# A two-stage kernel (a gated recurrence and a mixer): one group of small products a unit, keys' transposes ahead of products with v, and decays from one scan over logarithms from unit 6 on

## Chip, cores and metric

The kernel runs on one core of a Trainium2 chip. TensorE (PE, with its weight loads as PEld), VectorE (DVE), ScalarE (ACT), GpSimd (POOL) and SyncE (SP, which issues DMAs) each work through a queue of their own. The metric is the device time of one execution in microseconds. All data are float32.

## What is computed

The reference runs a gated outer-product recurrence over 768 steps for 4 batches and 8 heads of 48 channels, and puts its output, as a 768 x 384 matrix a batch, through a mixer:

```python
f = 1.0 / (1.0 + np.exp(-f_logit))
for t in range(S):
    state = f[:, :, t, :, None] * state + np.einsum('bhd,bhe->bhde', k[:, :, t], v[:, :, t])
    y[:, :, t] = np.einsum('bhd,bhde->bhe', q[:, :, t], state)
...
h = xt @ U @ V
u = x + h.transpose(0, 2, 1)
ch = np.maximum(u @ w_ch1, 0.0) @ w_ch2
return (u + ch)
```

## The kernel before

**Units.** Two heads make a unit, four units a batch, so units 0 to 15; unit n is in batch n // 4. The 768 steps are cut into 12 chunks of 64. Channels lie on partitions, head 0 at 0 to 47 and head 1 at 64 to 111. Within a chunk the recurrence becomes products: with decays X (from a step to the chunk's end) the keys become k·X, with Y = 1/X the queries become q·Y. These are the steps of a unit.

- `gates`, `keep`, `keys`, `read_back`, `queries` (function `prepare`, the "front") make f, X, k·X, Y and q·Y. `keep` is the backward scan at L876 on DVE over products of f, with a maximum (L883), a reciprocal (L884) and the chunk's whole decay (L886) behind it; `read_back` is the forward scan at L894. From unit 6 on (`TURNED`) f, k and q come in with channels in 32x32 blocks and are turned by DVE (L754); before that TensorE turns them (L777). Batch 0 has another way, from logarithms by products with a triangle (L835), which the change leaves as it is but for one copy.
- `kept` (function `attend`, the "rear") turns k·X back on TensorE (`pt`, L1002) and copies it to `kb` on ACT (L1006); `spread` copies the chunks' whole decays 48 times (L1012).
- `states` makes k·v a chunk (`ds`, L1026) and copies it to `added` on ACT (L1034); `scan` runs over the 12 chunks on DVE (L1051) and puts the states into `st`, on POOL (L1057) or ACT (L1055).
- `scores` makes k·q a chunk (`sc`, L975), masked on DVE to `A` (L988).
- `read` makes q·state (`y`, L1069); `inner` adds A·v to it (L1087) and ACT copies y into the mixer's x (L1093).

All of these products are small for TensorE: 48 or 64 rows and 48 to 128 columns of its array. A unit's y, ds, sc, pt (and others) are PSUM tiles of the pool `ps_big`, which has three buffers.

**The mixer.** One batch behind, the mixer's large products fill TensorE: `pz` (L300) with w_ch1, and with w_ch2 `po` (L355) in batch 0, `pw` (L389) with fewer products in the others, `pp` (L495) at the end. DVE makes the sums that these need (L204 in `add`, and L929 for sums of weights, at places given by `turns`).

**Order.** TensorE's order is the program's. `steps(first, last)` yields pieces of attention; before each piece a `Fill` emits its share of the mixer's pieces, so the number of pieces between two groups sets how many large products stand there. A piece made by `joined` runs several steps at once, with an empty piece ahead for each group of steps but one. Until the start of batch 2's mixing DVE's and ACT's orders are the program's as well; behind that, and for POOL throughout, a planner orders instructions by priority and by when they can start. The weights come in as 64-bit numbers and are converted on ACT (L91, L92), DVE (L98 to L100) and POOL (L101), one load beside each early piece of batch 1.

Before, a unit n has two groups: inner of n-2, scores of n-1 and kept of n together, and later read of n-1 and states of n together.

Of the kernel before, what the change touches and what calls it, by code (L numbers as in the profile page):

```python
# [564 lines left out]
def factored_path(ctx, tc, q, k, v, f_logit, moe_U, moe_V, moe_w_ch1, moe_w_ch2, out, ok):  # L565
# [154 lines left out]
    for i in range(2):  # L720
        nc.gpsimd.memset(wholes[i][:, 0:1], 0.0)
# [38 lines left out]
    def prepare(n):  # L760
# [5 lines left out]
        by_chunk = f[:, 0:S].rearrange("p (c t) -> p c t", t=C)  # L766
# [73 lines left out]
        def keep_logs():  # L840
# [16 lines left out]
            nc.scalar.copy(wholes[n % 2][:, 1:NCH], least[:, n, 1:NCH])  # L857

        def gates():
            f0 = T["f0"] = two.tile([P, NCH], F32, name="f0")  # L860
            if n < TURNED:
                pt = on_tensor("f")
                nc.scalar.activation(halves(f)[:, :, :, 1:C], pt[:, :, :, 1:C], AF.Sigmoid)
# [7 lines left out]
            nc.scalar.activation(by_chunk[:, :, 1:C], fv[:, :, 1:C], AF.Sigmoid)  # L871
            nc.scalar.activation(f0, fv[:, :, 0], AF.Sigmoid)

        def keep():
            X = T["X"] = late[:, 4, :]
            nc.vector.tensor_tensor_scan(  # L876
# [8 lines left out]
            whole = wholes[n % 2]  # L885
# [71 lines left out]
    def attend(n):  # L957
# [58 lines left out]

        def states():

            M = D if b else PAD
            ds = ps_big.tile([P, 2, 512], F32, name="ds", tag="big")  # L1020
            for c in range(NBL):
                for s in range(2):
                    for par in range(2):
# [3 lines left out]
                            ds[par * PAD : par * PAD + M, s, c * D : (c + 1) * D],  # L1027
                            lhsT=T["kb"][part[s ^ par], par, i, 0:M], rhs=vt[part[s ^ par], c, par, :],
# [3 lines left out]
            for r in rows if b else [slice(0, P)]:  # L1032
# [6 lines left out]
        def scan():  # L1039
# [8 lines left out]
            with tc.high_priority(offset=2 * AHEAD):  # L1048
                for e in halves_of(n):
                    of = slice(e.start * NCH, e.stop * NCH)  # L1050
                    nc.vector.tensor_tensor_scan(  # L1051
                        states[:, of], added[:, of], T["whole"].rearrange("p e c -> p (e c)")[:, of], 0.0, ALU.add, ALU.mult
# [46 lines left out]
        return [kept, states, scan, scores, read, inner, mask, spread]  # L1099
# [12 lines left out]
    def rear(n, *names):  # L1112
# [3 lines left out]
        if n not in here:  # L1116
            here[n] = dict(zip(("kept", "states", "scan", "scores", "read", "inner", "mask", "spread"), attend(n)))
# [10 lines left out]
    def steps(first, last):  # L1128

        def behind(n):  # L1130

            return HP + 3 <= n < NU - 1

        for n in range(first, last):
            if n < NU:
                yield from joined(rear(n - 2, "inner"), rear(n - 1, "scores"), rear(n, "kept"))
            else:
                for piece in rear(n - 2, "inner") + rear(n - 1, "scores"):
                    yield lambda: None
                    yield piece  # L1140
            if behind(n):
                yield from front(n, "read_back", "queries")
            if n + 1 < NU and n + 1 not in v_tiles:
                load(n + 1, "v")
            yield from front(n + 1, "gates", "keep", "keys")
            yield from joined(rear(n - 1, "read"), rear(n, "states", "scan"))
            if not behind(n + 1):
                yield from front(n + 1, "read_back", "queries")
            if n + 1 == last:
                yield from rear(n - 1, "inner")  # L1150
                if n + 2 < NU:
                    load(n + 2, "v")

# [160 lines left out]
    turns = 5, 7, 8, 13, 14, 15, 16, 18, 19, 22, 27  # L1314
# [6 lines left out]
    attention(pieces, Fill(todo[:-1], 33))  # L1321
# [373 lines left out]
```

## Time and profile before

| | |
|---|---|
| median of 3 runs | 466.35 us (465.92 to 467.19) |
| span of the profiled execution | 463.2 us |
| PE busy | 455.2 us, 98%, 5639 instructions |
| PEld busy | 394.5 us, 85% |
| DVE busy | 351.4 us, 76%, 585 instructions |
| ACT busy | 170.4 us, 37%, 323 instructions |
| POOL busy | 48.5 us, 10%, 56 instructions |
| granted TensorE clock, mean | 0.999 |

The span goes from the first to the last instruction of the profiled execution; the runs' times are of other executions and hold what lies around the span too. A busy PE is not PE at its peak: the ends of matmuls are modelled, and matmuls overlap, so the starts of rows say more than their lengths. In a timeline row stand the start, the length, the engine, the line, the operation, out<-in, shapes and the count of instructions merged; in brackets the idle time in front and what ended it. A float32 product is two instructions in the count, a transpose is one.

### The profile page before, as it was taken

The page shows a single profiled execution, that of the slowest core. Times are in us where ns is not written, and L with a number is a line of the kernel's source. Part 1 is how long each engine was busy: PE and PEld are TensorE (multiplying, and loading weights), DVE is VectorE, ACT ScalarE, POOL GpSimd, SP SyncE. Part 2 cuts the span into 40 slices and gives each one's busy share as a digit, 9 for nine tenths or more (in the row PEclk, how much of TensorE's full clock was granted, in tenths as well). Part 3 has the DMA queues.
Part 4 walks back from the last instruction along what each step waited for, and adds up shares of the span by engine and source line. Part 5 has one row for each costly group of instructions (what it writes and reads, how often), then busy time and mean ns, then how long its engine had stood idle before and what let it go on. Part 6 is the DMA issues. An engine that isn't in the chain of part 4 may idle for free.

```text
span 463.2 us, 13016 instructions
## 1 busy us (share of the span) xinstructions
PE 455.2 (98%) x5639; PEld 394.5 (85%) x5639; DVE 351.4 (76%) x585; ACT 170.4 (37%) x323; POOL 48.5 (10%) x56
## 2 busy tenths in 40 slices
PE   8999999999999999999999999999999999999997
PEld 5886888875666578999898888899989999999996
DVE  6778788979999677676765559977797887858652
ACT  6785776562333143323322323451412311212200
POOL 2002445634112001010000000000000000000000
PEclk9999999999999999999999999999999999999999
DMA  9959997577777604504633030100000000000001
GB/s 194 186 139 212 227 217 180 150 119 103 124 113 118 107 18 53 78 1 89 77 52 74 14 61 4 28 3 21 18 1 1 35 1 23 13 1 35 1 36 39
DMA packets 148583, 34.35 MB, mean 74 GB/s; under 512 B 136934, under 2 KB 146982, under 8 KB 148518
## 3 DMA queue, kind: packets, MB, share of 16 engines
q1 hardware_dynamic: 147718, 33.29, 37.1%
q8 instruction: 46, 0.75, 0.7%
q10 hardware_dynamic: 800, 0.15, 0.2%
q14 instruction: 19, 0.16, 0.1%
HBM read 28.70 MB, written 4.72 MB: 72 GB/s over the span
## 4 chain that ended last, share of the span: by engine, by line
PE 80%; DVE 11%; ACT 3%; DMA 2%; issue 2%; SPq 2%; DVEq 0%; ACTq 0%
PE pw L389 27%; PE pz L300 21%; PE pp L495 12%; PE po L355 5%; PE y L1069 2%; PE sc L975 2%; PE ds L1026 2%; PE y L1087 2%; PE pt L1002 1%; SPq L661 1%; DVE late L894 1%; PE pt L777 1%; DVE late L876 1%; PE pt L835 1%; DMA other<-in_f_logit_dram 1%
## 5 line engine op out<-in xcount | busy, mean ns | idle before, releaser
L300 PE MATMUL pz<-uT,w 128*128 128x256 f32 x492 | 111.5, 382 | 0.3
L300 PEld LDWEIGHTS pz<-uT,w 128*128 128x128 f32 x492 | 91.7, 190 | 12.9 <-ACT uT L289 0.6
L389 PE MATMUL pw<-zw,w_raw 128*128 128x192 f32 x216 | 38.0, 329 | 0.0
L389 PE MATMUL pw<-w,z_all 128*128 128x192 f32 x216 | 37.3, 327 | 0.0
L335 ACT ACTIVATE z_all<-pz 128x512 f32<-128x512 f32 x33 | 19.6, 598 | 45.1 <-PE pz L300 44.7
L389 PEld LDWEIGHTS pw<-w,z_all 128*128 128x128 f32 x216 | 35.3, 190 | 0.5
L389 PEld LDWEIGHTS pw<-zw,w_raw 128*128 128x128 f32 x216 | 35.1, 190 | 0.6 <-issue 0.3
L101 POOL TENSOR_TENSOR w<-w_y,w_r 128x384 int32<-128x384 int32 x24 | 31.5, 1311 | 37.0 <-DVE w_y L100 22.5
L876 DVE TENSOR_TENSOR_SCAN late<-fz,late 128x768 f32<-128x768 f32 x12 | 21.1, 1755 | 9.4 <-ACT fz L871 9.3
L488 ACT ACTIVATE other<-other 128x512 f32<-128x512 f32 x18 | 11.3, 630 | 40.3 <-DVE other L204 40.3
L355 PE MATMUL po<-w,zw 128*128 128x384 f32 x72 | 25.2, 495 | 0.0
L355 PE MATMUL po<-w,z_all 128*128 128x384 f32 x72 | 24.7, 493 | 0.0
L1057 POOL COPY st<-added 128x576 f32<-128x576 f32 x8 | 12.4, 1556 | 113.8 <-DVE added L1051 113.8
L988 DVE TENSOR_TENSOR A<-sc,causal 128x768 f32<-128x768 f32 x16 | 15.2, 953 | 8.5 <-PE sc L975 8.5
L355 PEld LDWEIGHTS po<-w,zw 128*128 128x128 f32 x72 | 13.2, 190 | 9.6 <-issue 0.8
L894 DVE TENSOR_TENSOR_SCAN late<-fz,other 128x768 f32<-128x768 f32 x12 | 21.0, 1750 | 0.2
L355 PEld LDWEIGHTS po<-w,z_all 128*128 128x128 f32 x72 | 13.3, 190 | 8.9 <-DVE o L204 0.6
L488 ACT ACTIVATE z_all<-z_all 128x512 f32<-128x512 f32 x12 | 7.6, 631 | 34.1 <-DVE z_all L204 34.1
L1034 ACT COPY added<-ds 48x576 f32<-48x576 f32 (+2 forms) x29 | 17.8, 619 | 4.5 <-PE ds L1026 4.1
L495 PE MATMUL pp<-v_nat,late 128*128 128x128 f32 x152 | 19.1, 275 | 0.0
L1069 PEld LDWEIGHTS y<-st,qT 48*64 48x64 f32 x704 | 13.6, 137 | 6.2 <-issue 4.5
L98 DVE TENSOR_SCALAR w_y<-w_y 128x384 f32<-128x384 f32 (+3 forms) x27 | 12.1, 449 | 8.8 <-ACT w_y L91 8.8
(233 smaller groups left out, 872.1 us busy)
## 6 DMA issues: line engine op xcount, KB each, us to landing
w_raw<-in_moe_w_ch_dram SPq DMA_DIRECT2D x18, 384.0 KB, 3.6
out_dram<-o SPq DMA_DIRECT2D x17, 192.0 KB, 1.9
v_nat<-in_v_dram SPq DMA_DIRECT2D x16, 144.0 KB, 3.8
v_nat<-in_v_dram SPq DMA_DIRECT2D x32, 72.0 KB, 3.5
zw<-in_moe_w_ch_dram SPq DMA_DIRECT2D x6, 384.0 KB, 5.1
out_dram<-o SPq DMA_DIRECT2D x14, 96.0 KB, 2.2
w<-in_k_dram SPq DMA_DIRECT2D x4, 288.0 KB, 4.1
w<-in_q_dram SPq DMA_DIRECT2D x4, 288.0 KB, 4.2
```

The source lines that it names most:

```text
L101: nc.gpsimd.tensor_tensor(dst.bitcast(I32), shaped(y.bitcast(I32)), shaped(r), ALU.add)
L300: nc.tensor.matmul(pm[:, i * 2 * P : (i + 1) * 2 * P], lhsT=w1[:, m, o : o + P], rhs=uT[a][:, m, :], start=(m == 0), stop=(m == NDC - 1))
L335: nc.scalar.activation(z[a, c][:, k : k + 2, :].rearrange("p i t -> p (i t)"), pm, AF.Relu)
L355: nc.tensor.matmul(pm, lhsT=z[a, i // NI][:, i % NI, s * P : (s + 1) * P], rhs=w2[:, i, :], start=(i == 0), stop=(i == NFC - 1))
L389: nc.tensor.matmul(W["pm"][:, n * HM : (n + 1) * HM], lhsT=lhs[:, i, :], rhs=rhs[:, i, :], start=(i == 0), stop=(i == NI - 1))
L488: nc.scalar.activation(dst, dst, AF.Relu, scale=float(SIGNS[n]))
L495: nc.tensor.matmul(pm[:, i, r * P : (r + 1) * P], lhsT=room["w"](wn)[:, r * P : (r + 1) * P], rhs=x_node(a, xn), start=((xn, wn) == of[0]) ...
L876: nc.vector.tensor_tensor_scan(backwards(X, S - 1, S), backwards(f, S, S), backwards(ends, S - 1, S), 0.0, ALU.mult, ALU.add,)
L894: nc.vector.tensor_tensor_scan(Y, f[:, 0:S], starts, 0.0, ALU.mult, ALU.add)
L988: nc.vector.tensor_tensor(T["A"], sc[:, :, 0 : NBL * C].rearrange("p h (c i) -> p h c i", i=C), causal.unsqueeze(1).unsqueeze(1).broadcast ...
L1034: nc.scalar.copy(added[r, 1:].rearrange("p (e c s) -> p e c s", c=NBL, s=2)[:, e], ds[r, :, 0 : NBL * D].rearrange("p s (c e) -> p e c s", ...
L1069: nc.tensor.matmul(o(c % 2, par, c // 2), lhsT=T["q"][rows[par], chunk[c]], rhs=T["st"][rows[par], c, :], start=(c <= 2), stop=False, skip ...
```

## The change

- In `steps`, unit n has one group: read of n-2, states and scan of n-1, scores of n-1, kept of n and inner of n-2, in this order, so kept (the keys' transposes) stands ahead of inner (products with v). The buffer of ds is taken ahead of that of y (`room_of_states`). The queries of n always come behind the group, then gates, keep and keys of n+1. In a batch's last round, read and inner of its last unit follow by themselves.
- In `states`, head 0's product is always 64 columns wide, head 1's 48 from batch 1 on, and one copy takes both heads to `added`.
- From unit 6 on, `gates` makes -log f (a maximum on POOL, DVE's transposes, Exp and Ln on ACT), `keep` sums it backward in one scan and takes X and the chunk's whole decay by Exp, and `read_back` takes Y by Exp: there is no second scan, maximum or reciprocal. Once, ahead of unit 6, four memsets set up what the scan needs (`within`).
- `whole` is one constant tile; its copy in `spread` leaves out the first chunk. `turns` has other places, and the last batch's `Fill` 38 portions for 33, as there are more pieces.

```diff
@@ gates, keep, read_back (prepare)
         def gates():
-            f0 = T["f0"] = two.tile([P, NCH], F32, name="f0")
             if n < TURNED:
+                f0 = T["f0"] = two.tile([P, NCH], F32, name="f0")
...
-            fT = late[:, 6, :]
-            turned(fT, r["f"])
+            if n == TURNED:
+                within()
+            g = f[:, 0:S]
+            nc.gpsimd.tensor_single_scalar(r["f"], r["f"], FLOOR, ALU.max)
+            turned(g, r["f"])
             follow("f")
-            fv = fT.rearrange("p (c t) -> p c t", t=C)
-            nc.scalar.activation(by_chunk[:, :, 1:C], fv[:, :, 1:C], AF.Sigmoid)
-            nc.scalar.activation(f0, fv[:, :, 0], AF.Sigmoid)
+            nc.scalar.activation(g, g, AF.Exp, scale=-1.0)
+            nc.scalar.activation(g, g, AF.Ln, bias=1.0)
+
+        def within():
+            nc.vector.memset(starts, 1.0)
+            nc.vector.memset(by_chunk(starts)[:, :, C - 1], 0.0)
+            for i in range(4, 6):
+                nc.vector.memset(by_chunk(late[:, i, :])[:, :, C - 1], 1.0)
 
         def keep():
             X = T["X"] = late[:, 4, :]
+            if n >= TURNED:
+                g = f[:, 0:S]
+                nc.vector.tensor_tensor_scan(
+                    backwards(g, S - 1, S), backwards(starts, S - 1, S), backwards(g, S - 1, S), 0.0, ALU.mult, ALU.add,
+                )
+                nc.scalar.activation(by_chunk(X)[:, :, 0 : C - 1], by_chunk(g)[:, :, 1:C], AF.Exp, scale=-1.0)
+                nc.scalar.activation(least[:, n, :], by_chunk(g)[:, :, 0], AF.Exp, scale=-1.0)
+                T["wholes"] = least[:, n, :]
+                return
...
         def read():
             Y = T["Y"] = late[:, 5, :]
+            if n >= TURNED:
+                nc.scalar.activation(by_chunk(Y)[:, :, 0 : C - 1], by_chunk(f[:, 0:S])[:, :, 1:C], AF.Exp)
+                return
@@ spread, states (attend)
         def spread():
-            whole = T["whole"] = one.tile([P, D, NCH], F32, name="whole")
-            nc.scalar.copy(whole, wholes[n % 2].unsqueeze(1).broadcast_to((P, D, NCH)))
+            nc.scalar.copy(whole[:, :, 1:], T["wholes"][:, 1:].unsqueeze(1).broadcast_to((P, D, NCH - 1)))
...
+        def room_of_states():
+            T["ds"] = ps_big.tile([P, 2, 512], F32, name="ds", tag="big")
+
         def states():
-            M = D if b else PAD
-            ds = ps_big.tile([P, 2, 512], F32, name="ds", tag="big")
+            M = [PAD, D if b else PAD]
+            if "ds" not in T:
+                room_of_states()
+            ds = T["ds"]
...
-                            ds[par * PAD : par * PAD + M, s, c * D : (c + 1) * D],
-                            lhsT=T["kb"][part[s ^ par], par, i, 0:M], rhs=vt[part[s ^ par], c, par, :],
+                            ds[par * PAD : par * PAD + M[par], s, c * D : (c + 1) * D],
+                            lhsT=T["kb"][part[s ^ par], par, i, 0 : M[par]], rhs=vt[part[s ^ par], c, par, :],
...
-            for r in rows if b else [slice(0, P)]:
+            for r in [slice(0, sum(M))]:
@@ steps
-        def behind(n):
-
-            return HP + 3 <= n < NU - 1
-
         for n in range(first, last):
-            if n < NU:
-                yield from joined(rear(n - 2, "inner"), rear(n - 1, "scores"), rear(n, "kept"))
-            else:
-                for piece in rear(n - 2, "inner") + rear(n - 1, "scores"):
-                    yield lambda: None
-                    yield piece
-            if behind(n):
-                yield from front(n, "read_back", "queries")
+            read = rear(n - 2, "read")
+            yield from joined(rear(n - 1, "room") + read if read else [], rear(n - 1, "states", "scan"),
+                              rear(n - 1, "scores"), rear(n, "kept") + rear(n - 2, "inner"))
+            yield from front(n, "read_back", "queries")
             if n + 1 < NU and n + 1 not in v_tiles:
                 load(n + 1, "v")
-            yield from front(n + 1, "gates", "keep", "keys")
-            yield from joined(rear(n - 1, "read"), rear(n, "states", "scan"))
-            if not behind(n + 1):
-                yield from front(n + 1, "read_back", "queries")
-            if n + 1 == last:
+            if n + 1 < last:
+                yield from front(n + 1, "gates", "keep", "keys")
+                yield lambda: None
+            elif n < NU:
+                yield from front(n + 1, "gates", "keep")
+                yield from rear(n - 1, "read")
+                yield from front(n + 1, "keys")
                 yield from rear(n - 1, "inner")
                 if n + 2 < NU:
                     load(n + 2, "v")
+            else:
+                for _ in range(4):
+                    yield lambda: None
+                yield from rear(n - 1, "read")
+                yield lambda: None
+                yield from rear(n - 1, "inner")
@@ last batch
-    turns = 5, 7, 8, 13, 14, 15, 16, 18, 19, 22, 27
+    turns = 6, 8, 9, 14, 15, 16, 17, 18, 20, 25, 29
...
-    attention(pieces, Fill(todo[:-1], 33))
+    attention(pieces, Fill(todo[:-1], 38))
```

More of the change, by code (lines that the diff above doesn't have):

```diff
@@ L1097, in inner @@
             del units[n], v_tiles[n]
-        return [kept, states, scan, scores, read, inner, mask, spread]
+        return [kept, states, scan, scores, read, inner, mask, spread, room_of_states]
     ahead, here = {}, {}
@@ L1116, in rear @@
         if n not in here:
-            here[n] = dict(zip(("kept", "states", "scan", "scores", "read", "inner", "mask", "spread"), attend(n)))
+            here[n] = dict(zip(("kept", "states", "scan", "scores", "read", "inner", "mask", "spread", "room"), attend(n)))
         return [here[n].pop(nm) for nm in names if nm in here[n]]
```

13 lines of the change are left out of this document (7 added, 6 removed).

## Prediction

> **What bounds the kernel now.** First the page's head and its chain, then busy time by stretch.
>
> ```profile
> span 463.2 us, 13016 instructions
> PE 80%; DVE 11%; ACT 3%; DMA 2%; issue 2%; SPq 2%; DVEq 0%; ACTq 0%
> 85.00:135.00 50.00, 49.21 (x793) 35.02 (x792) 44.71 (x61) 21.63 (x43) 15.56 (x10) 1.00 0.75 123
> 165.00:240.00 75.00, 74.85 (x995) 67.57 (x992) 53.69 (x68) 26.86 (x48) 3.63 (x3) 1.00 0.37 57
> 240.00:316.00 76.00, 75.85 (x1239) 66.91 (x1241) 55.20 (x89) 26.89 (x45) 0.00 (x0) 1.00 0.14 28
> ```
>
> The columns after the length are PE, PEld, DVE, ACT and POOL. TensorE is in work nearly without a hole (74.85 of 75 us, granted clock 1.00). So work taken from DVE alone is worth nothing from 165 us on; what counts there is how long TensorE takes for its row of instructions. Only between 85 and 135 us (batch 1) does DVE, at 44.71 of 50, come near, and TensorE has 0.79 us of holes.
>
> Next the timeline of PE, one unit in batch 2, and one line of the chain for the large products alone.
>
> ```profile
> 56.06 5.18 PE pz L300 x24
> 172.44 5.45 PE L300 MATMUL pz<-uT,w 128*128 128x256 f32 x24
> 177.81 0.84 PE L1069 MATMUL y<-st,qT 48*64 48x48 f32 x42
> 178.53 0.73 PE L1026 MATMUL ds<-v_nat,kb 64*48 64x48 f32 x45
> 179.19 5.45 PE L300 MATMUL pz<-uT,w 128*128 128x256 f32 x24
> 184.56 0.92 PE L1087 MATMUL y<-v_nat,A 64*64 64x48 f32 x48
> 185.30 0.89 PE L975 MATMUL sc<-qT,kz 48*64 48x64 f32 x48
> 186.12 0.59 PE L1002 MATMUL pt<-ident,kz 64*128 64x64 f32 x12
> 186.64 8.04 PE L300 MATMUL pz<-uT,w 128*128 128x256 f32 x36
> ```
>
> A unit meets two groups of small products: y with ds, then inner, sc and pt (kept). Twenty-four pz take 5.18 us by themselves, but 172.44 to 177.81 is 5.37: each group costs its neighbours 0.19 us.
>
> **The change part by part. First: one group.** I count groups of small products from the order of the steps. Before: 10 in batch 1 (the last y, ds and inner run together), 9 in batch 2, 9 in batch 3. After: 7, 6, 6. Nine boundaries go: 9 x 0.19 = -1.7 us. But each product's own time hangs on what stands behind it:
>
> ```profile
> 31.23 0.59 PE L1002 MATMUL pt<-ident,kz 64*128 64x64 f32 x12
> 31.75 0.92 PE L1087 MATMUL y<-v_nat,A 64*64 64x48 f32 x48
> 32.72 0.91 PE L1026 MATMUL ds<-v_nat,kb 64*64 64x48 f32 x48
> 33.45 0.89 PE L975 MATMUL sc<-qT,kz 48*64 48x64 f32 x48
> 251.88 0.91 PE L1087 MATMUL y<-v_nat,A 64*64 64x48 f32 x48
> 252.73 2.86 PE L300 MATMUL pz<-uT,w 128*128 128x256 f32 x12
> 312.39 0.86 PE L1069 MATMUL y<-st,qT 48*64 48x48 f32 x44
> 313.18 2.22 PE L389 MATMUL pw<-zw,w_raw 128*128 128x192 f32 x12
> ```
>
> From start to start: inner ahead of sc takes 0.74 (184.56 to 185.30), ahead of a large product 0.85 (251.88 to 252.73). In all twelve units inner now stands last; eight stood ahead of sc: 8 x 0.11 = +0.9. Head 0's ds becomes 64 columns wide instead of 48, so that one copy can empty it. A ds of 64 columns ahead of sc took 0.73 (32.72 to 33.45); one of 48 at its own group's end about 0.68 (178.53 to 179.19, with three strays ahead of it). Half at 64 and half at 0.73 x 48/64 is 0.64: 12 x -0.04 = -0.5. y ahead of ds takes 0.72 less those strays, 0.68; alone 0.79 (312.39 to 313.18): two more stand alone, +0.2. sc ahead of pt (185.30 to 186.12, 0.82) and pt (0.52) stay. Sum: -1.7 + 0.9 - 0.5 + 0.2 = **-1.1 us**. Bounds: +0.6 if the boundaries are worth nothing; -2.6 if inner's and y's rises don't come.
>
> pt now stands ahead of inner. In batch 0 that pair took 0.52 from start to start (31.23 to 31.75), as pt ahead of pz does (186.12 to 186.64), so I add nothing. The Trainium skill (TensorEngine Tiling, Key Properties) says that changing the tiling mode drains the engine, which speaks against this order: 64x128 tiles now stand between 64x64 ones. By it the eleven groups with pt would each pay up to a boundary's half, some 0.1 us, an estimate of +1.1 us for the sum; the 0.52 in both places does not show it.
>
> **A new wait in each group.** Three PSUM buffers hold ds, y and sc when pt needs one: it gets that of ds once ACT has copied it to added, with only sc between. Queued behind pt on TensorE: inner and all large products.
>
> ```profile
> 226.62 1.30 ACT L1034 COPY added<-ds 48x576 f32<-48x576 f32 x2 [0.46 <-PE ds L1026]
> L1034 ACT COPY added<-ds 128x576 f32<-128x576 f32 x3 | 1.9, 636 | 0.0
> ```
>
> Two copies of 1.30 become one of 0.64. It starts some 0.1 us after ds, while sc runs 0.82: pt is late by 0 to 0.1 us if ACT is free. I take 0.05 in 11 groups, **+0.5 us**. If an activation of 0.83 us stands in ACT's way, it is up to 0.8 each.
>
> **Stalls in batch 1 that go.** Three holes, each with its cause:
>
> ```profile
> 103.95 4.41 PE L355 MATMUL po<-w,zw 128*128 128x384 f32 x12
> 107.45 0.30 PEld L355 LDWEIGHTS po<-w,zw 128*128 128x128 f32 x2 [0.62 <-POOL w L101]
> 114.86 0.95 DVE L988 TENSOR_TENSOR A<-sc,causal 128x768 f32<-128x768 f32 x1
> 115.91 0.76 PE L1026 MATMUL ds<-v_nat,kb 64*48 64x48 f32 x48 [0.57 <-issue]
> 134.10 0.58 PE L1002 MATMUL pt<-ident,kz 64*128 64x64 f32 x12 [0.21 <-DVE kz L805]
> ```
>
> At 115.91 ds waited for sc's buffer, which the mask on DVE gave up at 115.81. At 107.45 the last weights were late because gates(6) stood ahead of their conversion on DVE; now it stands behind. At 134.10 keys were late. About 0.57 + 0.28 (the 4.41 of the po at 103.95, against 4.03 for as many at 98.62 below, less 0.1 for the boundary in front of it) + 0.21 = **-1.1 us**; bound 0.
>
> **Decays from logarithms.** From unit 6 on DVE loses a scan (L894), a max, a reciprocal, a copy and a product a unit; ACT gets four large activations and a small one in place of two; POOL gets a max over 128x768. From 165 us on TensorE's dense row hides all that. In batch 1 it does not: unit 6's gates have now to wait for the last weights' conversion, and its kept has only 8 portions of filling ahead instead of 9 behind an earlier start.
>
> ```profile
> 98.62 4.03 PE L355 MATMUL po<-w,z_all 128*128 128x384 f32 x12
> 99.89 0.36 DVE L98 TENSOR_SCALAR w_y<-w_y 128x384 f32<-128x384 f32 x1 [1.03 <-ACT w_y L91]
> 101.15 0.97 DVE L754 STREAM_TRANSPOSE late<-late 128x768 f32<-128x768 f32 x1
> L706 DVE MEMSET late<- 128x768 f32 x1 | 0.7, 698 | 0.2 <-issue 0.2
> L871 ACT ACTIVATE fz<-late 128x756 f32<-128x756 f32 x10 | 8.3, 832 | 20.2 <-DVE late L754 20.2
> L876 DVE TENSOR_TENSOR_SCAN late<-fz,late 128x768 f32<-128x768 f32 x12 | 21.1, 1755 | 9.4 <-ACT fz L871 9.3
> L805 DVE TENSOR_TENSOR kz<-kz,late 128x768 f32<-128x768 f32 x10 | 9.6, 958 | 0.3
> ```
>
> The conversion at 99.89 waits for ACT, which waits for TensorE's last pz of that loop. That pz ends 0.9 us earlier, since q's transposes (six of 128x128) move behind it and a boundary goes: 99.0. One conversion takes 1.26 (99.89 to 101.15): DVE does it, the product for q of unit 5 (0.96), the last conversion, memsets (0.70 and three small, 0.3) until 103.5; transpose 0.97, Exp and Ln on ACT 2 x 0.83, scan 1.76, transpose 0.97 (which hides the Exp for X), product 0.96: keys of unit 6 at **109.8**. TensorE comes to po at 98.4, does four portions of 2.03 (half of 98.62's row), then y, ds and sc (0.68 + 0.64 + 0.82), with 0.1 at the boundary: **108.7**. So a stall of 1.1 us, **+1.1 us**, behind which everything of TensorE queues. Bounds: nothing, if DVE is a microsecond ahead of this; 4.6 with what the second rival adds. Unit 7 has ten portions of filling between the groups, not eight, and no load of weights ahead of it: by the same steps it comes just in time.
>
> POOL's max is in no row. Its bounds are the memset's 0.70 on DVE and the join's pace, 1311 ns for 384 columns (L101 below), 2.6 us; I take 1.6, near the copy L1057's pace, and count it as hidden: f of unit 6 is there 20 us earlier, and POOL has gaps.
>
> ```profile
> L101 POOL TENSOR_TENSOR w<-w_y,w_r 128x384 int32<-128x384 int32 x24 | 31.5, 1311 | 37.0 <-DVE w_y L100 22.5
> L1057 POOL COPY st<-added 128x576 f32<-128x576 f32 x8 | 12.4, 1556 | 113.8 <-DVE added L1051 113.8
> 58.18 1.28 ACT L863 ACT_TABLE_LOAD   x1
> 59.47 0.80 ACT L863 ACTIVATE fz<-pt 128x756 f32<-128x756 f32 x1
> ```
>
> The way back from Sigmoid to Exp needs a table load. It took 1.28 us, and the activation followed at once; ACT is idle ahead of unit 6's transpose, so I count it as hidden. The Trainium skill (ScalarE: Activation LUTs, What ACT_TABLE_LOAD costs) adds a drain of about 1.38 us to each switch; no such gap stands between these two rows. By the page an unhidden switch would lengthen the stall by 2.7 us instead of 1.3, an estimate.
>
> **Sum.** -1.1 + 0.5 - 1.1 + 1.1 = -0.6 us on the span of 463.2. The median of the runs, 466.35, lies 3.15 us above that span; I leave that as it is: 465.7 us, less than 0.3% (1.4 us), about what a measurement of this kernel can tell from no change.
>
> **The rivals.** *The stall at kept(6) doesn't come* and the new wait is hidden: -1.1 - 1.1 = -2.2, 464.2 us; if inner's and y's rises fail too, 462.6. For it: DVE stood idle 1.03 us ahead of 99.89, so it has some reserve. Against: the chain behind the last conversion is serial.
>
> *Unit 6's gates come late* (the other side): POOL takes the max behind the last join (1.31) instead of ahead of it, which puts the transpose off by some 2.2 us, and Exp and Ln call for a table each, 1.28 more between them: stall 4.6, 469.2 us. From a stall of 1.7 on (keys of unit 6 at 110.4) the change gains nothing; from 3.1 on (111.8) it is slower by over 0.3%. Against: POOL's order is planned, and the max can go into a gap.
>
> *The group is held up by its own copy*: in batches 2 and 3 the planner orders ACT, and an Exp stands ahead of added in some of eight groups, a mean of 0.3 each: 468.1 us. Against: ACT is busy 26.86 of 75 us only.
>
> **Chances.** Forecast 0.46 (464.6 to 467.0, mostly within 0.3%), no stall 0.34, late gates 0.12, held by the copy 0.08. Faster by over 0.3%: 0.34 and an edge of the forecast, 0.37. Slower: 0.12, most of 0.08: 0.17. Within: 0.46. The range goes from 463.2, which leaves out the end of the first rival, to 468.1; the late gates lie above it.
>
> **What would show it.** Six groups in batches 2 and 3 each, a unit's group of some 3.5 us from y to pz; pt right behind sc (a hole over 0.1 us there speaks for the copy); a hole of about 1 us ahead of pt of unit 6 near 109 us, and none at the three places above. The forecast is wrong if TensorE has a hole over 2 us there, or new ones after 165 us.

## The result and the profile after

| | before | after |
|---|---|---|
| median of 4 runs each | 466.52 us (465.92 to 467.19) | 486.39 us (486.10 to 488.35) |
| ratio, with its 95% interval | | 1.0438 (1.0414 to 1.0461) |
| span of the profiled execution | 463.2 us | 486.6 us |
| granted TensorE clock, mean | 0.999 | 0.986 |

The change makes the kernel 20 us slower; 465.7 us had been predicted, with a range to 468.1. The profiled execution of after is the slowest of its four (488.35 us, clock 0.986; the others had 0.989 to 0.993), and that of before is shorter than its timed ones, so the two spans differ by 23.4 us where the medians differ by 20.

From the page of after, the head, busy times and the chain of waits:

```profile
span 486.6 us, 13041 instructions
PE 462.5 (95%) x5639; PEld 400.9 (82%) x5639; DVE 330.7 (68%) x539; ACT 212.1 (44%) x358; POOL 66.0 (14%) x65
...
PE 72%; DVE 10%; ACT 8%; issue 6%; DMA 2%; SPq 1%; POOL 1%; DVEq 0%; POOLq 0%; ACTq 0%
```

DVE has 21 us less to do, as meant, and ACT 42 us more. TensorE, which had 8.0 us without work in the whole span, now has 24.1, and it is 7.3 us longer busy with as many instructions. In the chain of work that ended last, ACT has gone from 3% to 8% and "issue" from 2% to 6%. In after, one of the stretches that the prediction shows of before, with busy PE, PEld, DVE, ACT and POOL and then the clock:

```profile
165.00:240.00 75.00, 71.02 (x824) 59.76 (x823) 41.34 (x46) 35.00 (x51) 10.55 (x6) 0.98 0.33 51
```

The dense row of TensorE from 165 us on, on which the prediction hid all of ACT's new work, has 4.0 us of holes in 75. Most of the larger holes in the timeline of PE:

```profile
113.95 0.59 PE L1024 MATMUL pt<-ident,kz 64*128 64x64 f32 x12 [4.23 <-DVE kz L807]
...
152.33 1.53 PE L1113 MATMUL y<-v_nat,A 64*64 64x48 f32 x48 [3.15 <-ACT seen L1102]
...
203.20 0.90 PE L1024 MATMUL pt<-ident,kz 64*128 64x64 f32 x12 [1.93 <-ACT added L1060]
...
228.27 0.58 PE L1024 MATMUL pt<-ident,kz 64*128 64x64 f32 x12 [0.96 <-ACT added L1060]
...
304.97 2.86 PE L300 MATMUL pz<-uT,w 128*128 128x256 f32 x12 [1.26 <-ACT z_all L335]
...
320.85 0.68 PE L1113 MATMUL y<-v_nat,A 64*64 64x48 f32 x30 [0.64 <-issue]
...
331.99 1.95 PE L389 MATMUL pw<-zw,w_raw 128*128 128x192 f32 x11 [1.20 <-issue]
```

Two kinds are seen: waits for something that ACT does or has done late, and holes, mostly in the middle of a row of products, that wait for nothing the profile knows (at 320.85 the 48 products with v are cut into 18 and 30). And behind a long hole the products themselves are slow: inner takes 1.53 us at 152.33 instead of 0.92. Short windows of after show the clock behind the three longest holes:

```profile
114.00:118.00 4.00, 4.00 (x64) 2.98 (x65) 3.77 (x5) 2.70 (x4) 1.20 (x1) 0.57 0.75 118
...
152.00:156.00 4.00, 3.67 (x52) 2.67 (x53) 2.44 (x3) 0.92 (x4) 0.00 (x0) 0.50 0.80 123
156.00:160.00 4.00, 4.00 (x10) 2.13 (x8) 0.00 (x0) 0.00 (x0) 0.00 (x0) 0.64 0.91 138
...
203.00:207.00 4.00, 3.80 (x64) 3.38 (x65) 4.00 (x5) 1.09 (x3) 1.13 (x1) 0.57 0.21 32
```

A window of 4 us at 0.57 gives 1.7 us less than one at full clock; the four together give 6.9, nearly all of the 7.3 by which TensorE is longer busy. The trace's own record of the clock agrees: it is at half from 114.49 to 117.90, from 152.04 to 158.86 and from 203.24 to 206.65 us, 13.65 us in all. So the 23.4 us of the two spans nearly add up, to 23.1: holes behind 48 us 15.0 more than before, clock 6.9, and batch 0 ends 1.2 later (a hole of 1.08 behind nothing at 25.80).

Why ACT is late is seen in its groups (count, then busy time and mean) and in its timeline at unit 6:

```profile
L876 ACT ACT_TABLE_LOAD x10 | 12.8, 1283 | 0.2
L891 ACT ACT_TABLE_LOAD x9 | 11.5, 1283 | 0.2
```

```profile
107.08 0.84 ACT L875 ACTIVATE fz<-fz 128x768 f32<-128x768 f32 x1 [3.09 <-DVE fz L754]
107.94 1.28 ACT L876 ACT_TABLE_LOAD   x1
109.24 0.84 ACT L876 ACTIVATE fz<-fz 128x768 f32<-128x768 f32 x1
110.10 1.28 ACT L891 ACT_TABLE_LOAD   x1
111.90 0.83 ACT L891 ACTIVATE late<-fz 128x756 f32<-128x756 f32 x1 [0.52 <-DVE fz L888]
...
149.48 1.28 ACT L891 ACT_TABLE_LOAD   x1
...
152.14 0.14 ACT L1102 COPY seen<-y 128x2 f32<-128x2 f32 x1
```

Ln at L876 and the Exp at L891 each call for a table of their own, in every unit from 6 on. The chain from f to the keys grows by 1.28 for Ln (the second load falls beside the scan), and all that stands behind in ACT's queue waits. The last two rows are the end of a later such stretch, from 146.47 us on: `seen`, the copy that lets inner go at 152.33, comes at 152.14, behind Exp, Ln and two loads. Ahead of the hole at 203.20 it is `added`, the copy that gives pt its buffer:

```profile
199.32 1.28 ACT L891 ACT_TABLE_LOAD   x1
201.13 0.83 ACT L891 ACTIVATE late<-fz 128x756 f32<-128x756 f32 x1 [0.53 <-DVE fz L888]
...
202.50 0.65 ACT L1060 COPY added<-ds 112x576 f32<-112x576 f32 x1
```

TensorE had been at sc, behind ds, from 200.36 on.

### The profile page after: what moved, and what is told of

Read it like the earlier page. It is cut to its first block, busy times and chain, and to the rows that moved or that the text cites. A ratio compares the mean times of both kernels' runs of the same rounds, so it can differ in the third digit from the quotient of the medians.

```text
span 486.6 us, 13041 instructions
## 1 busy us (share of the span) xinstructions
PE 462.5 (95%) x5639; PEld 400.9 (82%) x5639; DVE 330.7 (68%) x539; ACT 212.1 (44%) x358; POOL 66.0 (14%) x65
## 4 chain that ended last, share of the span: by engine, by line
PE 72%; DVE 10%; ACT 8%; issue 6%; DMA 2%; SPq 1%; POOL 1%; DVEq 0%; POOLq 0%; ACTq 0%
PE pw L389 24%; PE pz L300 19%; PE pp L495 11%; PE po L355 4%; PE y L1113 2%; PE y L1095 2%; ACT L876 2%; PE pt L1024 1%; PE ds L1052 1%; PE pt L779 1%; DVE fz L888 1%; ACT fz L876 1%; DVE fz L754 1%; PE pt L837 1%; DMA w<-in_q_dram 1%
## 5 line engine op out<-in xcount | busy, mean ns | idle before, releaser
L888 DVE TENSOR_TENSOR_SCAN fz<-other,fz 128x768 f32<-128x768 f32 x10 | 17.6, 1758 | 29.8 <-ACT fz L876 29.8
L101 POOL TENSOR_TENSOR w<-w_y,w_r 128x384 int32<-128x384 int32 x24 | 29.0, 1206 | 32.5 <-DVE w_y L100 20.7
L355 PE MATMUL po<-w,z_all 128*128 128x384 f32 x72 | 28.3, 547 | 0.6 <-ACT h L199 0.6
L1083 POOL COPY st<-added 128x576 f32<-128x576 f32 x8 | 10.3, 1292 | 127.0 <-DVE added L1077 115.3
L355 PEld LDWEIGHTS po<-w,z_all 128*128 128x128 f32 x72 | 14.9, 215 | 11.1 <-issue 3.2
L1113 PE MATMUL y<-v_nat,A 64*64 64x48 f32 x768 | 17.4, 237 | 5.2 <-ACT seen L1102 3.2
L204 DVE TENSOR_TENSOR w_raw<-z_all 128x768 f32<-128x768 f32 x12 | 11.4, 953 | 15.5 <-ACT z_all L335 14.1
L1077 DVE TENSOR_TENSOR_SCAN added<-added,whole 128x576 f32<-128x576 f32 x12 | 16.2, 1350 | 7.9 <-ACT added L1060 7.9
L1113 PEld LDWEIGHTS y<-v_nat,A 64*64 64x64 f32 x768 | 15.0, 150 | 7.9 <-ACT seen L1102 4.2
L875 ACT ACTIVATE fz<-fz 128x768 f32<-128x768 f32 x10 | 8.4, 842 | 26.1 <-DVE fz L754 26.1
```

Of the source, the lines that this page charges most:

```text
L101: nc.gpsimd.tensor_tensor(dst.bitcast(I32), shaped(y.bitcast(I32)), shaped(r), ALU.add)
L204: nc.vector.tensor_tensor(*args)
L355: nc.tensor.matmul(pm, lhsT=z[a, i // NI][:, i % NI, s * P : (s + 1) * P], rhs=w2[:, i, :], start=(i == 0), stop=(i == NFC - 1))
L888: nc.vector.tensor_tensor_scan(backwards(g, S - 1, S), backwards(starts, S - 1, S), backwards(g, S - 1, S), 0.0, ALU.mult, ALU.add,)
L1077: nc.vector.tensor_tensor_scan(states[:, of], added[:, of], whole.rearrange("p e c -> p (e c)")[:, of], 0.0, ALU.add, ALU.mult)
L1113: nc.tensor.matmul(o(s, par, c), lhsT=T["A"][part[s ^ par], par, c, :], rhs=vt[part[s ^ par], c, par, :], start=False, stop=True, skip_gro ...
```

## Experiments

Two theories stood first. **T**: the table loads are the loss, directly and through what waits behind them. **G**: the one group itself costs. Each of the first three kernels has one of them without the other, and the fourth has neither, only the logarithms. Where a difference of times is given below, it is of medians; each ratio is to the kernel before on the same chip (465.83 to 466.29 us on the four chips used).

### e1_preload: after without the loads

One line names a table set that has both functions, ahead of unit 6's Exp.

```diff
             if n == TURNED:
                 within()
+                nc.scalar.preload_act_table_set("natural_log_exp_and_others")
```

> The changed kernel with the table set that holds both Exp and Ln called once ahead of unit 6's gates; nothing else is altered. Theory T (tables): the 19 extra loads of 1.28 us, two in every unit from 6 on, made ScalarE's chain from gates to keys 2.6 us longer and held up copies that TensorE waits for; without them the time falls to 465 to 469 us. Rival G (the one group): the waits come from the group itself, from pt on the copy to added and from inner at its end; then 478 us or more stays.

478.44 us (478.23 to 478.93), ratio 1.0266 (1.0247 to 1.0285). Table loads are 3 instead of 23, ACT is busy 186.2 instead of 212.1 us. So the loads are worth 8.0 us, and 12 us are left: neither theory has it all (478.44 is above T's range and just inside G's). From PE's timeline and short windows:

```profile
112.94 0.91 PE L1025 MATMUL pt<-ident,kz 64*128 64x64 f32 x12 [2.79 <-DVE kz L807]
...
151.38 0.92 PE L1114 MATMUL y<-v_nat,A 64*64 64x48 f32 x48 [1.88 <-ACT seen L1103]
```

```profile
112.00:116.00 4.00, 3.06 (x61) 2.62 (x62) 4.00 (x5) 2.39 (x5) 1.20 (x1) 0.55 0.75 116
116.00:120.00 4.00, 4.00 (x9) 2.18 (x8) 2.11 (x3) 2.06 (x4) 0.00 (x0) 0.59 0.56 79
```

The first hole goes from 4.23 to 2.79 and the second from 3.15 to 1.88, 1.44 and 1.27 less, about one load each. Behind 2.79 the clock still halves; behind 1.88 it doesn't (inner takes 0.92 again).

### e2_groups: the one group without logarithms

After, with gates, keep and read-back of the kernel before (sigmoid, two scans).

```diff
-            nc.scalar.activation(g, g, AF.Exp, scale=-1.0)
-            nc.scalar.activation(g, g, AF.Ln, bias=1.0)
...
+            nc.scalar.activation(by_chunk(f[:, 0:S])[:, :, 1:C], fv[:, :, 1:C], AF.Sigmoid)
+            nc.scalar.activation(f0, fv[:, :, 0], AF.Sigmoid)
...
-            if n >= TURNED:
+            if False:
```

> The one group of the change with the decays of before (Sigmoid and two scans in every unit from 4 on), so no further table load. T: 463 to 468 us, and the holes ahead of pt and inner are below 1 us. G: 475 us or more, as the group is the cause.

473.43 us (472.64 to 473.75), ratio 1.0157 (1.0139 to 1.0176): 7.2 us over before, with the clock at 0.999, between the ranges of T and of G. G is right for about a third of the loss. PE is busy 455.7 us against 455.2, so what the group costs is holes. Those of PE's timeline from 100 us on that aren't at a batch's start:

```profile
110.73 0.59 PE L1022 MATMUL pt<-ident,kz 64*128 64x64 f32 x12 [1.46 <-DVE kz L807]
...
123.23 0.59 PE L1022 MATMUL pt<-ident,kz 64*128 64x64 f32 x12 [0.97 <-DVE kz L807]
...
192.17 0.80 PE L1111 MATMUL y<-v_nat,A 64*64 64x48 f32 x39 [0.18 <-issue]
...
241.65 0.45 PE L1111 MATMUL y<-v_nat,A 64*64 64x48 f32 x16 [0.92 <-issue]
...
305.25 0.68 PE L1111 MATMUL y<-v_nat,A 64*64 64x48 f32 x31 [0.24 <-issue]
...
316.06 2.11 PE L389 MATMUL pw<-zw,w_raw 128*128 128x192 f32 x12 [1.23 <-issue]
```

Keys late for units 6 and 7: 2.43 us. Holes behind nothing: 2.57. Another 2.17 stand in four waits for h, uT and o where a batch's mixing begins (0.57, 0.52, 0.29, 0.79). A group without a hole, in batch 2, is also longer than foreseen:

```profile
211.92 0.84 PE L1093 MATMUL y<-st,qT 48*64 48x48 f32 x42
...
213.25 0.91 PE L995 MATMUL sc<-qT,kz 48*64 48x64 f32 x46
214.25 0.59 PE L1022 MATMUL pt<-ident,kz 64*128 64x64 f32 x12
...
215.61 1.56 PE L300 MATMUL pz<-uT,w 128*128 128x256 f32 x6
```

It takes 3.69 us; pt starts 1.00 behind sc, not the 0.82 that sc takes, so the copy to added, which ends at 214.19, makes it 0.18 late. Six of the eleven groups with pt have this; in two the keys come later still, and in three, at a batch's start, there is no inner and pt is hardly late.

### e3_logs and e4_logs_preload: logarithms without the one group

The order, the widths of ds, its two copies and `turns` of before, with decays from logarithms; e4 has the line of e1 too. Against the kernel before:

```diff
+            g = f[:, 0:S]
+            nc.gpsimd.tensor_single_scalar(r["f"], r["f"], FLOOR, ALU.max)
+            turned(g, r["f"])
...
+            nc.scalar.activation(g, g, AF.Exp, scale=-1.0)
+            nc.scalar.activation(g, g, AF.Ln, bias=1.0)
```

> The order of steps, the widths of ds and its two copies as before, with the change's decays from logarithms and their table loads. T: clearly slower than before, 475 us or more, since the loads lengthen the chain in any order. G: within 2 us of before (466).

> As the run before it (order of before, decays from logarithms), with the table set for Exp and Ln called once ahead of unit 6. T: back within 3 us of before, 463 to 469. G: the same as without the call, within 1 us of it.

e3: 475.45 us (474.96 to 476.20), ratio 1.0198 (1.0176 to 1.0220). e4: 467.26 us (466.56 to 468.83), ratio 1.0028 (1.0016 to 1.0041). In the old order too the loads cost 8.2 us, some 3.4 of it as a clock at half for 6.83 us behind a hole of 3.17, and without them the logarithms cost 1.0. What is left in e4's timeline behind 100 us is a single hole:

```profile
110.61 0.91 PE L355 MATMUL po<-w,zw 128*128 128x384 f32 x2 [1.86 <-POOL w L101]
```

The last weights are late because unit 6's Exp and Ln (0.84 each) stand in ACT's queue ahead of their conversion at L91.

### e8_logs7: logarithms from unit 7 on

```diff
+    LOGS = TURNED + 1
...
-            if n >= TURNED:
+            if n >= LOGS:
```

> The kernel of e4_logs_preload (the order of before, decays from logarithms with the joint table loaded once) with logarithms only from unit 7 on; unit 6 keeps the sigmoid and its scans. In e4 po waited 1.86 us for the last weights: their conversion on DVE stood behind ACT, which did Exp and Ln of unit 6. Theory T (tables and that one wait are all that logarithms cost): the hole shrinks to the 0.3 to 0.6 of the kernel before, time 465 to 466.3, within 0.2% of before. Rival (logarithms cost more by themselves): 467 and more.

468.60 us (468.45 to 469.12), ratio 1.0050 (1.0030 to 1.0069), in the rival's range and 1.3 above e4. The wait for the last weights fell to 0.50 as expected, but inner at 124.08 us now waited 1.73 us for `seen`, behind unit 7's activations. The wait is moved to the next unit, not removed: in batch 1 ACT's added work doesn't fit ahead of these copies.

### e5_shift: are the unexplained holes the supply of instructions?

A count through the trace of e2 gave a new theory. PE's instructions (weight loads, products and its queue's own) are numbered from 0 by their start; beside the first one behind each hole stands the last packet of the instruction queue (page row below) that had started:

```profile
q8 instruction: 46, 0.75, 0.7%
```

```
hole ends (us)   instruction   = 193 + 256 k   packet starts   hole's end behind it
192.17           5313          k = 20          189.75          2.42
241.65           6593          k = 25          239.23          2.42
305.25           8385          k = 32          302.83          2.42
316.06           8897          k = 34          313.84          2.22
```

0.75 MB in 46 packets is 16 KB each, and 11,392 instructions are 248 a packet with the last one part full. All four holes end on the same place of a block of 256, and so do after's (6593, 8385, 8897); at the end of each exactly k packets of that queue have started. **Theory S**: PE gets its instructions in blocks of 256. Beside large products a block lasts long (48 instructions in 5.2 us); in the one group 402 instructions run in 3.69 us, so a block lasts 2.35, about the time from a packet's start to the hole's end. If a block begins 40 to 160 instructions into the group, its successor comes late. Shifting the stream must move the holes:

```diff
-        busy(3)
+        busy(1)
+        busy(27, 16)
```

> The kernel of e2_groups with one thing changed: two of the three idle products at the very start become 27 short ones, so that everything behind stands 100 instructions (weight loads and products counted) later in TensorE's stream, and takes the same time. In e2_groups the four holes of TensorE behind nothing that the profile shows (192.2, 241.7, 305.3, 316.1 us; 0.18, 0.92, 0.24, 1.23, together 2.57 us) each end at instruction 193 + 256 k of the stream, and 2.2 to 2.4 us behind the start of a 16 KB packet of the instruction queue. Theory S (instructions are brought in blocks of 256, and a group of 402 can run ahead of them when a block begins 40 to 160 instructions into it): the four holes go, since the blocks' ends now lie 224, 269, 180 to 241 and 280 instructions into those groups; one new hole of about 0.9 comes in the group of batch 2 near 212 us, where the end moves from 218 to 374; every hole of this kind again ends at 193 + 256 k. Time 471.0 to 472.3 us. Rival W (something in these products or in the groups' place, a wait that the profile doesn't show): the holes stay at the same products, time 473 to 474.

The time is 488.56 us (488.04 to 490.25), ratio 1.0487 (1.0459 to 1.0514), and was expected wrongly: the narrow idle products were not short (0.21 us each, 12.98 us instead of 4.21 for the row), and later in batch 0 the clock stood at 0.50 for 17.1 us (46.98 to 64.05), right behind a hole of 1.40 that ends at instruction 1729 = 193 + 256 x 6. These two, 8.8 us and half of 17.1, are nearly all of the 17.6 us by which pt of unit 6 comes later than in e2, and both are over at 70 us. The places answer the question. The four holes are gone; a new one stands where it was expected, in the group of batch 2 that had none (smaller than the 0.9 expected), and ends at instruction 6081 = 193 + 256 x 23. Another of 0.16 us, at 330.52, ends at 8897 again, where now other products stand:

```profile
46.83 0.59 PE L995 MATMUL sc<-qT,kz 48*64 48x64 f32 x11 [1.40 <-issue]
...
233.12 0.44 PE L1111 MATMUL y<-v_nat,A 64*64 64x48 f32 x14 [0.24 <-issue]
```

From pt of unit 6 (128.37 us here, 110.73 in e2) to the end of the span e5 takes 2.24 us less than e2, and the holes are 2.57 - 0.40 = 2.17 less. So it is shown that these holes follow the blocks of the instruction stream and not the products. That TensorE waits there for the block to arrive is what the packet 2.2 to 2.9 us ahead of each speaks for; no run changed the fetch itself.

### e6_two and e7_batch1: the group cut in two, and the old order in batch 1

Both start from e2. e6 puts portions of large products between ds and sc; e7 runs the steps of before in batch 1 (and has one portion fewer in the next batch's `Fill`).

```diff
-            yield from joined(rear(n - 1, "room") + read if read else [], rear(n - 1, "states", "scan"),
-                              rear(n - 1, "scores"), rear(n, "kept") + rear(n - 2, "inner"))
+            yield from joined(rear(n - 1, "room") + read if read else [], rear(n - 1, "states", "scan"))
+            yield from joined(rear(n - 1, "scores"), rear(n, "kept") + rear(n - 2, "inner"))
```

> The kernel of e2_groups with the one group cut in two, y, ds and the scan ahead of a portion or two of large products, then scores, keys' transposes and the products with v, as many pieces as before. Theory S (the group costs through its density): no group is longer than 216 instructions, so the holes behind nothing that the profile shows go (2.6 us), and the copy to added has two portions' time, so pt stands right behind sc (some 0.15 in 11 groups, 1.6 us); the boundaries come back (9 x 0.05, since a merged group with its boundary took 3.88 us against 3.84 for two). The late keys of units 6 and 7 (2.4 us) stay. Time 469 to 470.5 us. Rival O (it is the order around the group, the late states, keys and activations at the batch's ends, that costs): 472 to 474.

> The kernel of e2_groups with the order of the steps of the kernel before in batch 1 alone; batches 2 and 3 have the one group. Theory S: the waits of pt on the keys of units 6 and 7 (1.46 and 0.97 us) go, as they are not in the kernel before, and the rest of the cost stays with the two other batches: 470.5 to 471.5 us. Rival O (batch 1's order costs all of it, and what comes later follows from it): at most 468.

e6: 471.69 us (471.31 to 473.04), ratio 1.0123 (1.0099 to 1.0146); a miss by 1.2 us. Three of the four supply holes go. The fourth grows to 0.97, in a unit whose y, ds, sc, pt and inner follow each other without a large product between (300.53 to 305.43 us). 1.37 of the 2.43 us for late keys stay, but PE is busy 458.5 us instead of 455.7: the boundaries that come back cost 2.8 us, not the 0.5 expected. Its two groups, against those of before (1.37 and 2.08), and the hole that is left:

```profile
207.21 0.84 PE L1093 MATMUL y<-st,qT 48*64 48x48 f32 x42
...
208.67 2.22 PE L389 MATMUL pw<-zw,w_raw 128*128 128x192 f32 x12
...
212.76 0.93 PE L995 MATMUL sc<-qT,kz 48*64 48x64 f32 x48
...
214.98 3.29 PE L300 MATMUL pz<-uT,w 128*128 128x256 f32 x14
...
304.82 0.68 PE L1111 MATMUL y<-v_nat,A 64*64 64x48 f32 x31 [0.97 <-issue]
```

y with ds takes 1.46, and sc, pt and inner 2.22: 0.23 more a unit than before, before any merging.

e7: 472.48 us (471.56 to 473.31), ratio 1.0123 (1.0102 to 1.0145), 1.0 less than e2 where 2 to 3 were expected. Both waits on keys and all four at the batches' starts go, but pz waits 1.62 at 250.74 for a sum on DVE, and the four supply holes, at the same instructions, grow from 2.57 to 3.49. Batch 1's order isn't the whole; what makes the new wait was not pursued.

### e9_order, e11_order_narrow, e10_one_copy, e12_order_in_place: the order and the widths in the group

e9 has y, ds, inner, sc, pt; e11 also the narrow ds with two copies; e12 the order of e9 with as many pieces as e2; e10 is before with the wide ds and one copy.

```diff
# e9
-                              rear(n - 1, "scores"), rear(n, "kept") + rear(n - 2, "inner"))
+                              rear(n - 2, "inner"), rear(n - 1, "scores") + rear(n, "kept"))
# e12
+                              rear(n - 2, "inner") + rear(n - 1, "scores"), rear(n, "kept"))
# e10, in before
-            M = D if b else PAD
+            M = [PAD, D if b else PAD]
-            for r in rows if b else [slice(0, P)]:
+            for r in [slice(0, sum(M))]:
```

> The kernel of e2_groups (the one group, decays from sigmoids and scans) with the products with v again ahead of scores and keys' transposes: y, ds, inner, sc, pt. Theory P (a group's length is set by what stands beside what): pt has 1.6 us instead of 0.8 behind ds, so its wait for the copy to added (0.18 in 11 groups) goes; inner stands ahead of sc, not of a large product (0.11 in 11); pt of units 6 and 7 comes 0.85 later, so 1.7 us of its waits on keys go; the holes of the instruction supply stay where the stream has them, 2.6 us. Group of batch 2 3.4 us instead of 3.69, time 468 to 470 us, against 473.4 of e2_groups. Rival Q (the order inside costs nothing, the group's length is what it is): 472.5 to 474.

> The kernel of e9_order with head 0's ds 48 columns wide again and two copies to added instead of one. Theory P: y and ds take 1.37 us together as in the kernel before instead of 1.46, 11 times, and the two copies of 1.30 have 1.6 us of products ahead of pt, or just not: 1 us less than e9_order, 467 to 469. Rival (the prediction's own term, a ds of 64 columns is the shorter one, and the second copy makes pt late): at or above e9_order.

> The kernel before with one thing of the change: head 0's ds 64 columns wide, and one copy to added over 112 rows instead of two over 48. Theory P (the wide form costs 0.09 a unit, and ACT's relief is hidden behind TensorE): 1.0 us slower, 466.8 to 467.8 us. Rival (the prediction's term of -0.5, 0.04 a unit): 465.3 to 466.

> The order of e9_order (y, ds, inner, sc, pt in one group), but with as many pieces as e2_groups has, so that each group keeps the place among the large products that it has in e2_groups; e9_order had moved them, and left a hole of 3.47 us at the end of a batch, which is to go here. Theory S+P: the group takes 3.4 us instead of 3.69; pt of units 6 and 7 waits less for its keys (0.6 to 1.4 us less each); but a group that is run faster overtakes the instruction supply by more, at the same instructions of the stream (5313, 6593, 8385, 8897, and 7873 as in e9_order): the holes behind nothing that the profile shows are 5 to 6.5 us together instead of 2.57. Time 470 to 473 us: what the order wins is given to the supply. Rival (the supply is no limit, the holes of e9_order came from the moved groups): the holes stay at 2.6 or less, and the time is 468 to 470.

e9: 483.15 us (481.09 to 486.04), ratio 1.0351 (1.0318 to 1.0384). e11: 482.95 us (482.38 to 485.82), 1.0381 (1.0343 to 1.0418). Both were expected under 470. The group is as short as foreseen (3.39 us), but the edit left out a piece in rounds without an inner, so groups moved among the large products, a batch's last sums came late, and e9's clock was at half for 13.65 us:

```profile
224.08 15.91 PE L300 MATMUL pz<-uT,w 128*128 128x256 f32 x60 [3.47 <-DVE o L204]
```

So e9 and e11 say little of the order. e12 holds the places:

```profile
191.72 0.68 PE L995 MATMUL sc<-qT,kz 48*64 48x64 f32 x27 [0.95 <-issue]
...
211.88 0.84 PE L1093 MATMUL y<-st,qT 48*64 48x48 f32 x42
...
215.26 5.02 PE L300 MATMUL pz<-uT,w 128*128 128x256 f32 x22
...
241.03 0.33 PE L995 MATMUL sc<-qT,kz 48*64 48x64 f32 x5 [1.27 <-issue]
...
304.87 0.56 PE L995 MATMUL sc<-qT,kz 48*64 48x64 f32 x19 [1.04 <-issue]
...
316.38 0.27 PE L995 MATMUL sc<-qT,kz 48*64 48x64 f32 x1 [1.56 <-issue]
```

473.33 us (472.63 to 473.99), ratio 1.0154 (1.0129 to 1.0179), just above the 470 to 473 expected: no faster than e2, though its group takes 3.38 us (211.88 to 215.26) instead of 3.69. The four holes stand at the same instructions (5313, 6593, 8385, 8897) and are 4.82 us instead of 2.57. A denser group overtakes its supply by more: 2.25 us of what the order wins go to the supply. The waits on keys were expected to shrink at both units by 0.6 to 1.4; they were 0.75 and 1.10, 0.58 less together, and the second grew.

e10: 466.70 us (466.28 to 470.30), ratio 1.0019 (1.0001 to 1.0038), just under what Theory P expected and above the rival's range. y with ds takes 1.46 us where before it took 1.37, and PE is busy 456.8 us, 1.6 more than before:

```profile
285.33 0.84 PE L1069 MATMUL y<-st,qT 48*64 48x48 f32 x42
...
286.79 2.86 PE L300 MATMUL pz<-uT,w 128*128 128x256 f32 x12
```

No kernel tried is faster than the one before.

## Why the prediction was wrong

**The step that failed** is the table load, "counted as hidden": "The way back from Sigmoid to Exp needs a table load". It was priced once, at 1.28 us, with the right duration; the trace of after has 20 loads more than that of e1, because Ln and the Exps of one unit ask for different tables. The second rival had "a table each, 1.28 more between them" as part of a chance of 0.12, for unit 6 alone. Taking the loads away gives 8.0 us in the one group (e1) and 8.2 in the old order (e4 against e3). With it fell "from 165 us on TensorE's dense row hides all that": in after pt waits 1.93 us at 203.20 for `added`, behind an Exp and its load.

This is not the whole of it. Without the loads e1 still takes 478.44 us, and e2, which has neither loads nor logarithms, 473.43; both lie above the range's end at 468.1. The other 12 us lie in the terms below that were too small or missing, and in what arises only when both parts stand together.

The Trainium skill (ScalarE: Activation LUTs, Table sets: the hidden batching unit) lists a set that holds both exp and ln and counts one load for ln followed by exp. By after's profile (10 and 9 loads) that set isn't taken by itself; by e1's, where it was named, the page's count holds. The prediction has the price of a load but counts one switch where each unit makes two.

The other terms, with what they measured:

| term | predicted | measured |
|---|---|---|
| boundaries that go | -1.7 us | -2.8 (PE busy, e6 to e2) |
| inner last, ds wide, y alone | +0.6 | +2.1 (ds 11 x 0.09, pt and inner 8 x 0.14, e10 and e6) |
| pt waits for the copy to added | +0.5 | +1.1 (6 x 0.18, e2) |
| three stalls of batch 1 go | -1.1 | gone from e2's timeline |
| keys of unit 6 late | +1.1 | 1.46 in e2, 2.79 in e1, 4.23 in after |
| keys of unit 7 | just in time | 0.97 late in e2 |
| instruction supply | not in the sum | 2.57 in e2, 2.14 in after |
| starts of the batches | not in the sum | 2.17 in e2 |

- **Boundaries**: right in sign, too small.
- **Inside the group**: the sign of ds was wrong. It was taken from a ds ahead of sc in batch 0 (0.73) and set against 0.68; e10 measures the wide form by itself, 0.09 longer a unit, not 0.04 shorter. With pt and inner 0.14 more and the copy's 0.18, the group takes 3.69 us, not 3.5, and with its one boundary 3.88 against 3.83 for the two groups before: the merge wins nothing even where TensorE has no hole. The lower bound of this part, -2.6, was summed wrongly: without the rises of inner and y its terms give -2.2, and the first rival's end is 463.0, not 462.6.
- **The copy**: "late by 0 to 0.1 us if ACT is free" was 0.18, and where ACT wasn't free (the third rival, 0.08) after shows 1.93 and 0.96.
- **Keys of unit 6**: the wait was foreseen, the size was not: with the joint table it is 2.79 us (e1), and e2's 1.46 is with sigmoids. The list of DVE's work ahead of unit 6's transpose has two conversions and one product; it leaves out read-back's scan for unit 5, which now stands there as the queries always come behind the group. From e2:

```profile
98.50 1.75 DVE L914 TENSOR_TENSOR_SCAN late<-fz,other 128x768 f32<-128x768 f32 x1
```

  The last pz of the loop also ended no earlier than before (its activation starts at 98.74 us in e2, 98.82 before), and the conversions took 1.5 to 2.0 us, not 1.26. So DVE began the transpose at 106.36 in e1, not at 103.5; from there to the keys it took 6.4 us, much as the forecast's 6.3. The 4.23 of after lies inside the bounds given (0 to 4.6), and a hole over 2 us there, or new ones after 165, was the sign named beforehand for a wrong forecast.
- **Supply, clock and batch starts** were in no term. The measured terms of the group (with e2's 1.46 for unit 6 and the three stalls at -1.1) sum to 6.5 us, beside 7.7 between the spans of e2 and before; 1.2 us have no term.

Together: the group costs 7.2 us (e2), the logarithms 1.0 (e4); both without loads cost 12.2 (e1), so 4.0 arise only together, of which 3.4 are the clock behind the longer wait on unit 6's keys (two windows at 0.55 and 0.59). The loads bring it to 20.

What stays open: why the waits at the batches' starts come with the new order (in e7, with batch 1's old order, they are gone), and why removing one wait in batch 1 brought another in e7 and e8.

## What to carry to other kernels

When a change alternates two functions on ACT, count a table load at every switch until a trace shows otherwise, and name the joint set. Before merging rows of tiny products, compare the time in which TensorE runs 256 of its instructions with the 2.2 to 2.9 us from a packet's start to the hole's end here: groups that ran a block in 2.35 us (e2) or less stopped at its end for up to 1.56 us. A hole of 2 us can cost nearly as much again in clock behind it (1.93 and 1.7 us in after), so price a stall by more than its length.

## What the hardware showed unexpectedly

**Instruction supply.** The 31 holes of 0.15 us and more behind nothing that the nine kernels with the one group (after, e1, e2, e5, e6, e7, e9, e11 and e12) have from 165 us on all end at instruction 193 + 256 k, 2.2 to 2.9 us behind the start of a 16 KB packet; the kernels in the old order have none there. The Trainium skill (Runtime: NRT & Kernel Launch, Instruction fetch mechanics) gives blocks of 16 KiB or 256 instructions, which agrees, and calls crossing a block mostly hidden; here crossings cost up to 1.56 us each (e12), which disagrees for rows of some 110 instructions a us (402 in 3.69 us).

**The clock.** Behind the holes of 1.93, 3.15 and 4.23 us in after and of 2.79 in e1 the granted clock fell to 0.50 to 0.64 in windows of 4 us, for 3.41 or 6.83 us by the traces' record of the clock; behind 1.86 (e4) and 1.88 (e1) it didn't. It isn't a fixed length: behind 2.90 us in e11 the clock stayed at 1.00, and in e5 it fell behind 1.40. The Trainium skill (TensorE: Matmul & The Clock Gate, Part 1) puts the fall behind an idle window of about 3.4 us; of the falls named here only that behind 4.23 us follows a hole as long. In every trace the changes of the clock lie whole multiples of 3.41 us apart. On these steps the 1.93 us of after lie within one step, and the 2.90 of e11 across the edge of two (1.26 and 1.64); that this decides it is not shown.

**Table loads.** Each took 1.283 us, and where the next activation had nothing else to wait for, it followed within 0.04 us.
